# Attention then a bilinear feed-forward on one core: the first batch's softmax is normalised after the value product instead of before it

## The chip, the core and the metric

The kernel runs on one core of a Trainium2 chip. The core has a matrix engine (PE, with its weight loads shown as PEld), a vector engine (DVE), a scalar engine (ACT), a general engine (POOL) and a queue engine (SP) that issues most transfers. The metric is the device time of one execution in microseconds (us). PE reads the on-chip memory and writes only PSUM; DVE and ACT bring results from PSUM back.

## The reference

```python
scores = q @ k.T / sqrt(64); decay = cum[:, None] - cum[None, :]      # cum = cumsum(log(f))
attn = exp(scores + decay - max), with the causal mask
attn = attn / (attn.sum(-1) + 1e-9)
x = attn @ v                          # 8 batches, 8 heads, 576 rows, 64 per head
out = ((x @ w_a) * (x @ w_b)) @ w_out # 4608 tokens, 512 -> 1536 -> 512
```

Inputs and outputs are float32, and the kernel computes in float16 with float32 sums.

## The kernel before

The work is cut into head pairs: `t` counts them from 0 to 31, four to a batch, so `t = 0` to `3` is batch 0 and `4` to `7` batch 1. Rows of a head are in five blocks `i` (four of 128 and one of 64). For each `t` and `i` the steps are:

- PE makes scores (`qk_group`), DVE takes their row maximum (`do_max`, L488; from batch 3 on `do_decay`), ACT the exponential with its row sum (`do_exp`, L550 and L544 for `i = 4`) into the tiles PA and PB (P), some of which lie in tiles of other names (`spread`, `S`);
- DVE makes the reciprocal of the sum (`do_recip`, L559 and L557, kept in `st`), and POOL multiplies P by it, one instruction for each head and block (`do_norm`, L567);
- P is transposed: in batch 0 by PE (`pe_tr`, L591, with an eviction by DVE or ACT), in the others by a DMA from SP's queue (`do_tr`, L583). PE multiplies by V (`do_pv`, L623; `do_pv4`, L636, for block 4), and DVE or ACT evicts the result into `xT` (`do_ev`, `do_ev4`).

The transposed tile has the keys on the partitions and the rows of the softmax along its free axis. Beside this stands the feed-forward, by runs of tokens: `psa` and `psb` (the gate products, L874), a copy of one (ACT or DVE), their product `ht` on DVE (L890), and the output `pso` (L899). The weights come in pieces by DMAs that POOL issues (L365): first 512 columns of `w_a` and of `w_b`, then 1024 of each (the large pieces), then `w_out`. The fifth gate product, `psa` of block 4 of the first run, is the first that needs the large piece of `w_a`.

Nothing is scheduled while it runs: every step is one `op` with its dependencies, `ORDER` lists all of them in a hand-over order, and `CHOICE` gives the engine of those that may go to several. Each engine executes its instructions in that order; so an instruction that waits holds up all behind it on its engine, loads and weight DMAs among them. Rings of tiles bound how far ahead a step may go: 4 PSUM tiles `ff` for all products but the scores, 3 tiles `n32` for loaded inputs, 2 tiles `osb` for outputs. Forty `fill` steps put matmuls without use on PE.

## Time and profile before

| what | before |
|---|---|
| time of the runs | 402.16 us median of 3 (401.61 to 402.33) |
| profiled execution: span from first to last instruction | 400.7 us |
| instructions | 11076 |
| PE, DVE busy in the span | 383.2 us (96%), 315.3 us (79%) |
| POOL, ACT busy | 253.6 us (63%), 250.0 us (62%) |
| mean granted PE clock | 0.986 |

The profile is of one execution, whose span is the only time known of it. It has several views: busy time of each engine in a stretch, with granted clock (1.00 is full) and the mean busy share of the 16 DMA engines (above 1 where transfers overlap); who waited for whom, with total, count and longest wait; groups of instructions by line and shape with busy total and mean duration in ns; the instructions in order of time (start, duration); and the chain of work that ended last. Matmul ends are modelled, so spacing says more of them than duration.

### The profile page before, as it was taken

The numbers are of one execution on the slowest core, as the hardware profiler recorded it, in microseconds if no ns is written. First come the engines' busy times: TensorE is split into PE (matmuls) and PEld (weight loads), VectorE is DVE, ScalarE is ACT, GpSimd is POOL, SyncE is SP. The second block draws the span as 40 slices with busy tenths as digits, with TensorE's granted clock in tenths as the row PEclk, the third lists the DMA queues.
The fourth block names the chain that finished last, engine by engine and source line by source line (L and its number), as shares of the span: only waits on it lengthen the run. The fifth ranks groups of instructions, "written<-read, shape, count | busy, mean of one in ns | idle before, by whom it ended". The sixth has DMA issues, their size and how long they took to land.

```text
span 400.7 us, 11076 instructions
## 1 busy us (share of the span) xinstructions
PE 383.2 (96%) x4040; PEld 212.0 (53%) x4040; DVE 315.3 (79%) x907; ACT 250.0 (62%) x757; POOL 253.6 (63%) x424
## 2 busy tenths in 40 slices
PE   8598799998999999999999999999999999999996
PEld 7466576765855544454445454544444444444553
DVE  8989798976778988997988889898969892373560
ACT  5798766666667778758785777577868673300011
POOL 3889876887397876897896849787968553000000
PEclk9889999998999999999999999999999999999999
DMA  7999989989999999999999999999997729000102
GB/s 282 240 186 289 204 177 224 213 150 215 208 301 208 227 171 330 201 277 212 295 187 286 211 255 273 233 241 190 276 187 218 157 66 202 28 2 36 71 0 79
DMA packets 148311, 78.22 MB, mean 195 GB/s; under 512 B 130592, under 2 KB 133408, under 8 KB 148256
## 3 DMA queue, kind: packets, MB, share of 16 engines
q1 hardware_dynamic: 144272, 72.53, 77.4%
q0 software_dynamic: 3696, 4.72, 7.0%
q8 instruction: 31, 0.51, 0.5%
q10 hardware_dynamic: 288, 0.26, 0.2%
q14 instruction: 24, 0.20, 0.1%
HBM read 49.69 MB, written 9.58 MB: 148 GB/s over the span
## 4 chain that ended last, share of the span: by engine, by line
PE 79%; DMA 9%; DVE 4%; POOL 2%; ACT 2%; issue 2%; SPq 0%; POOLq 0%; DVEq 0%; ACTq 0%
PE pso L899 22%; PE psa L874 22%; PE psb L874 21%; PE sc L401 8%; DMA wa<-in_moe_w_a_dram 5%; PE pv L611 2%; DVE st L488 2%; DMA k<-in_k_dram 1%; PE pv L613 1%; PE sc L636 1%; DMA PTB<-spread 1%; DMA PTB<-PB 1%; DVE qT L302 1%; PE pv L623 1%; ACT PB L550 1%
## 5 line engine op out<-in xcount | busy, mean ns | idle before, releaser
L874 PE MATMUL psa<-xT,wa 128*128 128x512 f16 (+2 forms) x528 | 116.2, 343 | 2.3 <-DMA wa<-in_moe_w_a_dram 1.7
L874 PE MATMUL psb<-xT,wb 128*128 128x512 f16 (+2 forms) x528 | 116.2, 343 | 0.1
L899 PE MATMUL pso<-wout,ht 128*128 128x512 f16 (+1 forms) x444 | 98.4, 374 | 0.0
L567 POOL TENSOR_SCALAR PA<-PA,st 128x128 f16<-128x128 f16 (+2 forms) x162 | 76.0, 482 | 31.8 <-DVE st L559 20.4
L890 DVE TENSOR_TENSOR ht<-psb,a 128x512 f16<-128x512 f32 (+2 forms) x132 | 76.2, 589 | 22.0 <-PE psb L874 15.0
L512 DVE CUSTOM_DVE_ANT_0 S<-sc,spread 128x128 f32<-128x128 f32 (+3 forms) x160 | 86.7, 567 | 7.7 <-PE sc L401 5.4
L138 ACT CAST a<-psa 128x512 f16<-128x512 f32 (+2 forms) x85 | 43.5, 515 | 55.9 <-PE psa L874 53.8
L874 PEld LDWEIGHTS <-wa 128*128 128x128 f16 x528 | 50.1, 99 | 45.5 <-issue 3.7
L874 PEld LDWEIGHTS <-wb 128*128 128x128 f16 x528 | 50.4, 99 | 41.5 <-issue 1.7
L567 POOL TENSOR_SCALAR PB<-PB,st 128x512 f16<-128x512 f16 (+1 forms) x84 | 58.7, 712 | 15.7 <-DVE st L559 14.6
L550 ACT ACTIVATE PA<-S,st 128x256 f16<-128x256 f32 (+2 forms) x120 | 59.9, 502 | 12.5 <-DVE st L512 12.4
L899 PEld LDWEIGHTS <-ht 128*128 128x128 f16 x444 | 41.7, 98 | 46.8 <-issue 1.3
L488 DVE TENSOR_REDUCE st<-sc 128x2 f32<-128x512 f32 (+7 forms) x68 | 46.3, 723 | 6.0 <-PE sc L401 5.3
L401 PE MATMUL sc<-kT,qT 32*128 32x128 f16 (+5 forms) x960 | 41.7, 272 | 5.5 <-ACT PA L550 2.1
L550 ACT ACTIVATE PB<-S,st 128x512 f16<-128x512 f32 x40 | 28.5, 714 | 7.9 <-DVE st L512 7.9
L401 PEld LDWEIGHTS <-qT 32*128 32x128 f16 (+1 forms) x960 | 18.6, 96 | 26.7 <-issue 14.4
L142 DVE CAST a<-psa 128x512 f16<-128x512 f32 (+2 forms) x47 | 26.2, 560 | 7.2 <-PE psa L874 6.6
L559 DVE RECIPROCAL st<-st 128x2 f32<-128x2 f32 x128 | 18.5, 157 | 14.0 <-ACT PA L550 8.7
L142 POOL CAST k<-k 128x1152 f16<-128x1152 f32 (+1 forms) x15 | 20.5, 1367 | 8.9 <-DMA k<-in_k_dram 8.9
L138 ACT COPY osb<-pso 128x512 f32<-128x512 f32 (+1 forms) x22 | 12.4, 570 | 19.9 <-PE pso L899 15.1
L138 ACT CAST xT<-pv 128x512 f16<-128x512 f32 (+2 forms) x39 | 17.0, 446 | 11.8 <-PE pv L636 5.8
L140 POOL TENSOR_SCALAR q<-q 128x1152 f16<-128x1152 f32 (+1 forms) x15 | 20.6, 1372 | 5.0 <-DMA q<-in_q_dram 4.2
(98 smaller groups left out, 491.5 us busy)
## 6 DMA issues: line engine op xcount, KB each, us to landing
spread<-cum_d SPq DMA_DIRECT2D x20, 576.0 KB, 5.9
out_dram<-osb SPq DMA_DIRECT2D x35, 256.0 KB, 3.8
q<-in_q_dram SPq DMA_DIRECT2D x15, 576.0 KB, 7.3
k<-in_k_dram SPq DMA_DIRECT2D x15, 576.0 KB, 5.2
v<-in_v_dram SPq DMA_DIRECT2D x32, 256.0 KB, 6.1
wout<-in_moe_w_out_dram POOLq DMA_DIRECT2D x3, 512.0 KB, 8.7
v<-in_v_dram SPq DMA_DIRECT2D x8, 128.0 KB, 7.2
wb<-in_moe_w_b_dram POOLq DMA_DIRECT2D x1, 1024.0 KB, 13.5
```

What stands on the lines that cost most here:

```text
L138: nc.scalar.copy(out=out_, in_=in_)
L140: ENG[e].tensor_scalar(out=out_, in0=in_, scalar1=0.125, scalar2=1.0, op0=MUL, op1=MUL)
L142: ENG[e].tensor_copy(out=out_, in_=in_)
L401: nc.tensor.matmul(out=dst, lhsT=lhsT, rhs=rhs, start=start, stop=stop, skip_group_check=True)
L488: nc.vector.tensor_reduce(out=m if i == 4 else st[:, 2 * i:2 * i + 2][:, h:h + 1] if isinstance(x, list) else m, in_=y, axis=AXX, op=MAX, ...
L512: nc.vector.tensor_tensor_reduce(out=o, in0=x, in1=y, scale=-1.0, scalar=3e38, op0=ADD, op1=MIN, accum_out=m)
L550: nc.scalar.activation(out=p_blocks(t, i)[:, :, h, :], in_=x.rearrange("p (j k) -> p j k", k=128), func=EXP, scale=sign, bias=st[:, c:c + ...
L559: nc.vector.reciprocal(out=st[:, 20 + 2 * i:22 + 2 * i], in_=st[:, 10 + 2 * i:12 + 2 * i])
L567: ENG[e].tensor_scalar(out=p, in0=p, scalar1=st[:, c:c + 1], scalar2=1.0, op0=MUL, op1=MUL)
L874: nc.tensor.matmul(out=o, lhsT=w16[:, db, 128 * fb:128 * fb + 128], rhs=tokens(db, t0, n), start=(db == 0), stop=(db == 3))
L890: nc.vector.tensor_tensor(out=ht[:, 0:n], in0=T.pop(("psb", t0, fb))[:, 0:n], in1=T.pop(("a16", t0, fb))[:, 0:n], op=MUL)
L899: nc.tensor.matmul(out=o, lhsT=T[("ht", t0, fb)][:, 128 * tb:128 * tb + 128], rhs=wout16[:, fb, c], start=(fb == 0), stop=(fb == 11))
```

## The change

Only batch 0 (`RAW = 1`) changes in what it does. Its P is transposed and multiplied by V as the exponential left it. The 36 multiplications on POOL go. In their place, for each head pair and each of two groups of rows (blocks 0 and 1; blocks 2, 3 and 4):

- the reciprocals are split into a float16 high part and the rest (`rhi`, `rlo`, 4 or 5 columns; POOL, DVE or ACT);
- PE carries them across (`rmm`, 8 matmuls for the first group and 12 for the second): a column of reciprocals, repeated 64 times, times the unit matrix, so that every partition holds the reciprocals along the free axis; the two parts are added in PSUM, in a tile of the ring `ff`;
- ACT or DVE copies that to a tile `rb` of the ring `osb` (`rev`);
- the eviction of the value product becomes a multiplication by `rb`, on DVE alone (`ever`, `ev4r`).

The filler is one matmul over 512 columns in place of four over 128. `ORDER` and `CHOICE` are new for the first third: from the step after the third output run on (position 894 of 2311 before, 890 of 2307 now; on PE the last `psa` of the run of tokens from 768) all steps stand in the same order on the same engines. Ahead of it, loads, weights and steps of batches 0 to 2 have other places, and 36 steps another engine.

```diff
+    r16 = fixed("r16", [128, RAW * NP, 2, 10])
...
-        for n in range(4):
-            nc.tensor.matmul(out=p[:, 128 * n:128 * n + 128], lhsT=ident, rhs=ident, start=True, stop=True)
+        nc.tensor.matmul(out=p.rearrange("p (n k) -> p n k", n=4), lhsT=ident,
+                         rhs=ident.unsqueeze(1).to_broadcast([128, 4, 128]), start=True, stop=True)
...
+    def recip_high(e, t, lo, hi):
+        cast(e, r16[:, t, 0, lo:hi], T[("st", t)][:, 20 + lo:20 + hi])
+
+    def recip_low(e, t, lo, hi):
+        ENG[e].tensor_tensor(out=r16[:, t, 1, lo:hi], in0=T[("st", t)][:, 20 + lo:20 + hi], in1=r16[:, t, 0, lo:hi], op=SUB)
+
+    def across(t, rows):
+        o = T[("psr", t, rows[0])] = ps.tile([128, 512], FP32, tag="ff", bufs=RING["ff"], name="psr")
+        for i in rows:
+            c = slice(128 * (i - rows[0]), 128 * (i - rows[0]) + (64 if i == 4 else 128))
+            for e in range(2):
+                for h in range(2):
+                    r, x, n = (HP[h], 64 * h, 8) if i == 4 else (slice(0, 128), 0, 2 * i + h)
+                    nc.tensor.matmul(out=o[HP[h], c], lhsT=r16[r, t, e, n:n + 1].to_broadcast([r.stop - r.start, 64]),
+                                     rhs=ident[r, x:x + c.stop - c.start], start=i == rows[0] and e == 0, stop=e == 1,
+                                     skip_group_check=True)
+
+    def across_evict(e, t, rows):
+        n = 320 if 4 in rows else 256
+        x = T[("rb", t, rows[0])] = osb_pool.tile([128, 512], FP32, tag="osb", name="rb")
+        cast(e, x[:, 0:n], T.pop(("psr", t, rows[0]))[:, 0:n])
...
-        cast(e, xT[pr][:, b, c], T.pop(("pv", t, rows))[:, c])
+        o = T.pop(("pv", t, rows))
+        if b < RAW:
+            nc.vector.tensor_tensor(out=xT[pr][:, b, c], in0=o[:, c], in1=T[("rb", t, rows[0])][:, 0:256], op=MUL)
+        else:
+            cast(e, xT[pr][:, b, c], o[:, c])
...
+            if b < RAW:
+                norms.setdefault((t, part), []).extend((i, ex) for ex in es)
+                pair = (0, 1) if i < 2 else (2, 3, 4)
...
+                continue
             for h in range(1 if i == 4 else 2):
                 nm = op("P", f"norm{i}", lambda e, i=i, h=h: do_norm(e, t, i, h), [rc])
...
     ORDER = """
-        42-44 0 20 41 2 1 64 26 31 23 54 55 45 16 32 13 12 71 46 37 47 56 18 67 27 65 34 72 73 68 48 24 19
```

What stood in POOL's queue before around the large pieces (`wb16` and `wa16` with 1024 columns; PA and `spread2` are multiplications of P, `nv1` a cast of batch 1's V):

```order
L567 TENSOR_SCALAR PA_353<-PA_353,st_341 128x2x128 x2
L365 DMA wa16_70<-in_moe_w_a_dram 128x4x512
L567 TENSOR_SCALAR PA_374<-PA_374,st_370 128x2x128 x2
L365 DMA wb16_71<-in_moe_w_b_dram 128x4x512
L567 TENSOR_SCALAR PA_374<-PA_374,st_370 128x128
L142 CAST nv1_74<-v32_377 128x1024
L567 TENSOR_SCALAR spread2_80<-spread2_80,st_444 128x2x128
L365 DMA wb16_71<-in_moe_w_b_dram 128x4x1024
L365 DMA wa16_70<-in_moe_w_a_dram 128x4x1024
```

The same place now (`r16` holds the split reciprocals, `q16` and `k16` are batch 1's casts):

```order
L367 DMA wa16_70<-in_moe_w_a_dram 128x4x512
L144 CAST nv0_73<-v32_439 128x1024
L577 TENSOR_TENSOR r16_75<-st_364,r16_75 128x4
L144 CAST r16_75<-st_291 128x4
L577 TENSOR_TENSOR r16_75<-st_358,r16_75 128x4
L367 DMA wb16_71<-in_moe_w_b_dram 128x4x512
L144 CAST r16_75<-st_257 128x4
L577 TENSOR_TENSOR r16_75<-st_257,r16_75 128x4
L142 TENSOR_SCALAR q16_629<-q32_444 128x1152
L367 DMA wb16_71<-in_moe_w_b_dram 128x4x1024
L144 CAST k16_697<-k32_695 128x1152
L367 DMA wa16_70<-in_moe_w_a_dram 128x4x1024
```

The two large pieces now stand behind the split reciprocals of all four head pairs and behind a cast each.

SP's queue before, from the sixth transfer on (batch 0's V, then batch 1's and the first of batch 2):

```order
L288 DMA q_332<-in_q_dram 128x1152
L272 DMA v_355<-in_v_dram 128x8x64 x2
L272 DMA v_377<-in_v_dram 128x8x64 x2
L272 DMA v_380<-in_v_dram 128x8x64 x2
L288 DMA k_384<-in_k_dram 128x1152
L272 DMA v_690<-in_v_dram 64x8x64
L231 DMA cum_d<-cum_f 64x576
L288 DMA k_932<-in_k_dram 128x1152
L288 DMA q_1035<-in_q_dram 128x1152
L288 DMA q_1050<-in_q_dram 128x1152
```

And now (`k_414` is the second half of batch 1's k, `k_932` before; `q_1232` the first half of batch 2's q, `q_1035` before):

```order
L274 DMA v_278<-in_v_dram 128x8x64 x2
L290 DMA k_414<-in_k_dram 128x1152
L274 DMA v_439<-in_v_dram 128x8x64 x2
L290 DMA q_444<-in_q_dram 128x1152
L274 DMA v_564<-in_v_dram 64x8x64
L290 DMA k_695<-in_k_dram 128x1152
L274 DMA v_720<-in_v_dram 64x8x64
L233 DMA cum_d<-cum_f 64x576
L274 DMA v_1082<-in_v_dram 128x8x64 x2
L290 DMA q_1098<-in_q_dram 128x1152
L290 DMA q_1232<-in_q_dram 128x1152
```

The second half of batch 1's k moved ahead of three loads, the first half of its V behind four, and batch 2's q behind both.

DVE's queue before, where the first four value products are evicted (`psP` are transposes):

```order
L488 TENSOR_REDUCE st_370<-sc2_576 128x2
L559 RECIPROCAL st_444<-st_444 128x2
L142 COPY xT3_69<-psP_626 128x768
L142 COPY xT0_66<-psP_647 128x768
L142 COPY xT2_68<-psP_654 128x768
L559 RECIPROCAL st_341<-st_341 128x2
L559 RECIPROCAL st_437<-st_437 128x2
L559 RECIPROCAL st_341<-st_341 128x2
L142 CAST xT3_69<-pv_675 128x256
```

And now:

```order
L490 TENSOR_REDUCE st_291<-sc2_489 128x2
L577 TENSOR_TENSOR r16_75<-st_291,r16_75 128x4
L490 TENSOR_REDUCE st_257<-sc2_490 128x2
L144 COPY rb_544<-psr_535 128x256
L144 COPY xT2_68<-psP_547 128x768
L668 TENSOR_TENSOR xT1_67<-pv_570,rb_544 128x256
L668 TENSOR_TENSOR xT3_69<-pv_589,rb_566 128x256
L144 COPY xT0_66<-psP_598 128x768
```

A transpose's eviction went to ACT, a split and a copy of carried reciprocals came, and the evictions of values became products.

More of the change, by code (lines that the diff above doesn't have):

```diff
@@ L71 @@
     EARLY = 2
+    RAW = 1
     T = {}
@@ L641, in do_ev @@
         c = slice(128 * rows[0], 128 * rows[-1] + 128)
-        cast(e, xT[pr][:, b, c], T.pop(("pv", t, rows))[:, c])
+        o = T.pop(("pv", t, rows))
[3 more added lines that the diff above has]
+            cast(e, xT[pr][:, b, c], o[:, c])
     def do_ev4(e, t):
         b, pr = divmod(t, NP)
-        cast(e, xT[pr][:, b, SF:S], T.pop(("pv4", t)))
+        o = T.pop(("pv4", t))
+        if b < RAW:
+            nc.vector.tensor_tensor(out=xT[pr][:, b, SF:S], in0=o, in1=T[("rb", t, 2)][:, 256:320], op=MUL)
+        else:
+            cast(e, xT[pr][:, b, SF:S], o)
     last_row = [[] for _ in range(RING["bc"])]
+    raw = {}
     ev_ops, late, last_pb = {}, {}, [[] for _ in range(RING["PB"])]
@@ L721, in softmax @@
             st_users[t].extend(es + [rc])
+            if b < RAW:
+                norms.setdefault((t, part), []).extend((i, ex) for ex in es)
+                pair = (0, 1) if i < 2 else (2, 3, 4)
+                raw.setdefault((t, pair), []).append(rc)
+                if len(raw[(t, pair)]) < len(pair):
+                    continue
+                x = (2 * pair[0], 9 if 4 in pair else 4)
+                rh = op("PDA", "rhi", lambda e, x=x: recip_high(e, t, *x), raw[(t, pair)], x[1] - x[0])
+                rl = op("PD", "rlo", lambda e, x=x: recip_low(e, t, *x), [rh], x[1] - x[0])
+                st_users[t].extend([rh, rl])
+                rm = op("E", "rmm", lambda _, pair=pair: across(t, pair), [rh, rl, o_id], 320 if 4 in pair else 256)
+                ru = take(rm, "ff")
+                re_ = op("AD", "rev", lambda e, pair=pair: across_evict(e, t, pair), [rm], 320 if 4 in pair else 256)
+                ru.append(re_)
+                raw[(t, pair[0])] = re_, take(re_, "osb")
+                continue
             for h in range(1 if i == 4 else 2):
@@ L845, in values @@
             pvu = take(pv, "ff")
-            ev = op("DA", "eve", lambda e, rows=rows: do_ev(e, t, rows), [pv])
+            ev = op("D" if b < RAW else "DA", "ever" if b < RAW else "eve", lambda e, rows=rows: do_ev(e, t, rows), [pv])
+            if b < RAW:
+                ev.deps.append(raw[(t, rows[0])][0])
+                raw[(t, rows[0])][1].append(ev)
             pvu.append(ev)
@@ L853, in values @@
         us = take(pv4, "ff")
-        ev4 = op("DA", "ev4", lambda e: do_ev4(e, t), [pv4])
+        ev4 = op("D" if b < RAW else "DA", "ev4r" if b < RAW else "ev4", lambda e: do_ev4(e, t), [pv4])
+        if b < RAW:
+            ev4.deps.append(raw[(t, 2)][0])
+            raw[(t, 2)][1].append(ev4)
         us.append(ev4)
@@ new lines @@
+        234 235 132 133 262 263 167 212 213 107 108 4 52 220 272 273 53 248 249 221 92 182-184 150 190 191
+        1594-1596 268 269 1598 1600 185 216 217 168 91 87 270 88 186 187 1597 1599 1601 1602 1604 197-199
+        205 206 3 173 178 286 180 63 179 174-176 299 305 300 301 307 154 287 293 1603 207 1606 1605 1608
+        1607 1609 214 215 218 242 219 288 295 243 94 230 289 181 306 222 294 188 93 224 336 189 278 225 231
+        308 1610 302 1611 1612 337 1614 338 223 1613 1616 172 343 1615 339 1618 1620 1619 1622 1621 344 256
@@ new lines @@
+        458 1699 473 461 476-478 414 504 506 420 1651 421 505 360 1700 1701 479 1702 1703 335 455 495 411
+        355 434 415 451 329 433 412 462 482 483 418 1705 1706 510 511 1707 452 463 419 484 1708 507 323 424
+        436 437 512 354 486 427 401 428 405 386 435 440 441 438 439 488 514 1710 457 1711 1714 1715 1712
+        1713 487 489 1716 1718 1719 1722 1720 380 515-517 1721 1723 1724 524 1725 474 536 537 502 1717 1726
+        1728 381 426 431 425 429 430 459 468 564 570 432 481 480 469 1727 1730-1732 1729 1733-1737 503 538
```

81 lines of the change are left out of this document (43 added, 38 removed), and 119 rows, old and new, of the table ORDER.

## Prediction

> **What bounds the kernel now.** First the page and busy time by stretch: which engine is full, and where.
>
> ```profile
> span 400.7 us, 11076 instructions
> ```
> ```profile
> core 0: us, PE busy (x) PEld busy (x) DVE busy (x) ACT busy (x) POOL busy (x), PEclk, DMA share, GB/s
> 0.00:44.20 44.20, 33.20 (x563) 26.24 (x563) 39.72 (x101) 33.56 (x107) 33.85 (x61) 0.92 1.01 248
> 44.20:62.00 17.80, 17.76 (x288) 12.81 (x289) 15.52 (x29) 12.06 (x35) 12.58 (x19) 1.00 0.96 188
> 62.00:92.00 30.00, 29.16 (x480) 20.38 (x482) 25.95 (x67) 20.68 (x76) 24.59 (x42) 1.00 1.03 193
> 92.00:100.00 8.00, 6.22 (x88) 4.63 (x82) 4.13 (x9) 4.90 (x14) 5.10 (x10) 0.79 1.10 210
> 100.00:137.20 37.20, 36.75 (x501) 23.75 (x501) 29.96 (x83) 25.66 (x87) 26.90 (x43) 1.00 1.07 240
> 137.20:310.00 172.80, 172.75 (x1559) 80.69 (x1558) 151.61 (x506) 126.75 (x375) 134.84 (x225) 1.00 1.00 237
> 310.00:390.00 80.00, 80.00 (x528) 39.27 (x527) 47.78 (x115) 24.86 (x65) 15.71 (x28) 1.00 0.31 72
> ```
>
> At 137.2 stand the last feed-forward products of the part whose order changes; all behind it keeps its order. There PE is busy for 172.75 of 172.80 us and then 80.00 of 80.00, at full clock: the tail is matmul time alone, and it shifts as a block with PE's arrival at it. So the change is worth what it does to PE before 137.2. There PE idles 11.0 us up to 44.2 and 3.1 behind (0.04, 0.84, 1.78, 0.45), and from 92 to 100 its clock is 0.79, which costs 0.21 x 8 = 1.7 us more. Up to 44.2 no engine is full, but DVE is the nearest (39.72 of 44.20, and its first microsecond waits for the program's start); POOL with its 33.85 has room. Who ends PE's waits:
>
> ```profile
> PE sc L401 <- ACT PA L550: 2.1, 1, 2.1
> PE sc L401 <- DVE st L559: 2.1, 1, 2.1
> PE pv L636 <- DMA PTB<-spread: 1.8, 1, 1.8
> PE psa L874 <- DMA wa<-in_moe_w_a_dram: 1.7, 1, 1.7
> PE pv L636 <- DVE st L488: 0.8, 1, 0.8
> ```
>
> No wait ends at POOL's multiplication (L567), though POOL's work is what the change removes. The chain that ended last says the same: it runs through DVE's transposes and maxima, then through one weight transfer, and from there along PE.
>
> ```profile
> 22.51 21.65 DMA wa<-in_moe_w_a_dram
> 44.21 0.61 PE psa L874 x4
> ```
>
> **The change part by part.**
>
> *POOL's multiplications of the first batch go: 36.*
>
> ```profile
> L567 POOL TENSOR_SCALAR spread<-spread,st 128x128 f16<-128x128 f16 x4 | 1.5, 376 | 0.8 <-DVE st L559 0.8
> L567 POOL TENSOR_SCALAR spread<-spread,st 128x576 f16<-128x576 f16 x2 | 1.5, 744 | 0.9 <-DVE st L557 0.9
> ```
>
> The smallest took 0.376 and the largest 0.744; at their mean, 0.56, that is 20 us of POOL. All of it lay beside DVE and ACT, so by itself it is worth nothing on the end: DVE is late next.
>
> *Term A: the start of the fifth gate product (44.21).* POOL also issues the weights, and their place in its queue moves.
>
> ```profile
> 21.95 0.16 DVE L559 RECIPROCAL st<-st 128x2 f32<-128x2 f32 x1
> ```
> ```profile
> 21.71 0.81 POOL L365 DMA_DIRECT2D wb<-in_moe_w_b_dram  x1
> 22.51 0.75 POOL L365 DMA_DIRECT2D wa<-in_moe_w_a_dram  x1
> ```
> ```profile
> L142 POOL CAST k<-k 128x1152 f16<-128x1152 f32 x2 | 2.8, 1395 | 0.0
> ```
>
> Before, the two large pieces go out at 21.71 and 22.51. Now POOL first waits for the last reciprocal of rows 0 and 1 (ends at 22.1 by the row above), does some four tiny operations on it (taken at 0.15 each, like the reciprocal; POOL's smallest row, 0.376, would add 0.9), the small wb piece (0.8), and a q cast (1.4): wb's large piece at 22.1 + 0.6 + 0.8 + 1.4 = 24.9, 3.2 later. Behind it a k cast of 1.4 and the issue of 0.8: wa's large piece at 27.1, 4.6 later. Against that stand the loads in its way.
>
> ```profile
> q1 hardware_dynamic: 5108, 3.63, 39.4%
> ```
> ```profile
> 28.25 0.35 SPq L288 DMA_DIRECT2D k<-in_k_dram  x1
> 31.86 3.51 SPq L288 DMA_DIRECT2D q<-in_q_dram  x2
> ```
>
> From 14 to 46 us the loads' queue takes 39.4% of 32 us for 3.63 MB, 3.5 us a MB, so 2.0 us for a load of 0.59 MB. Three such loads start during wa's 21.65 us. SP's new order has one of them (batch 1's second k) ahead of all weights, and one (batch 2's q) behind batch 1's v and q: two leave, 4.1 us. Landing: 44.16 + 3.2 - 4.1 = 43.3, if the weights' queue works in order; ends: 40.1 (the loads leave and the later issue costs nothing) and 27.1 + 21.65 = 48.8 (the transfer keeps its length). I take 43.3, since queue and loads together fill the DMA engines (share 1.01 in the first row of the stretches).
>
> Does PE arrive by then? Its last row before the wait, and two groups from the chain behind it:
>
> ```profile
> 42.12 0.44 PE L591 MATMUL psP<-ident,PB 128*128 128x128 f16 x5
> ```
> ```profile
> 45.26 0.69 PE sc L401 x28
> 46.49 0.28 PE pv L636 x10
> ```
>
> PE is done at 42.56. The new order puts a score group (0.69) and a value group (0.28) ahead of the fifth gate product, and moves one transposition group (about 0.44) behind it: 0.53 more done. DVE up to there loses a subtraction and a q cast, two evictions of transposes and three casts of values, and gains a transpose and the products:
>
> ```profile
> L302 DVE STREAM_TRANSPOSE kT<-k 128x576 f32<-128x576 f32 x8 | 9.7, 1214 | 0.0
> L220 DVE TENSOR_TENSOR wout<-cum_f,wout 32x320 f16<-32x320 f32 x1 | 1.0, 1035 | 0.0
> L140 DVE TENSOR_SCALAR q<-wout 128x512 f16<-128x512 f32 x1 | 1.2, 1158 | 0.0
> L142 DVE COPY xT<-psP 128x768 f16<-128x768 f16 x7 | 3.7, 546 | 0.0
> L142 DVE CAST xT<-pv 128x256 f16<-128x256 f32 x6 | 2.4, 408 | 0.0
> L890 DVE TENSOR_TENSOR ht<-psb,a 128x256 f16<-128x256 f32 x36 | 14.7, 418 | 6.5 <-ACT a L138 2.6 <-PE psb L874 2.5 <-PE pv L623 0.6
> ```
>
> Gone: 1.04 + 1.16 + 3 x 0.41 and about 1.2 for two evictions (0.55 and a larger one), 4.6. Come: 1.21, five products of PSUM and SBUF, priced by the feed-forward's product of the same size (0.42; the last is shorter), one copy of 0.4, three tiny ones of 0.15 and one eviction of 0.5: 4.6. No gain and no loss; a product with a float32 second operand stands in no row, and lies between the cast (0.41) and double that. The first four products also wait for copies of the carried reciprocals, three of them queued on ACT between exponentials; behind them on DVE stand the maxima of row 4, and for those PE's first feed-forward products leave time. PE then arrives at 42.56 + 0.53 = 43.1 and starts at 43.3: 0.9 earlier with 0.53 more behind it, **A = -1.4** (ends -1.6 with no wait, +4.1 with 48.8).
>
> *Term B: the matmuls that carry the reciprocals across.* For each head pair 8 and 12; 44 stand ahead of the fifth gate product, in the stretch where PE idles 11 us, and cost nothing while it does (36 ns each, 1.6 us, if that cover goes). 36 stand behind it, on the full PE.
>
> ```profile
> 65.37 0.51 PE pv L623 x14
> 108.25 0.43 PE sc L636 x20
> 80.34 0.22 PE idle L178 x4
> ```
>
> Values products of the same shape (64 output rows, 128 columns) take 0.51 / 14 = 36 ns each; with 64 columns 22 ns; a full 128 x 128 one in the filler 55 ns. **B = 36 x 36 ns = +1.3** (0.8 to 2.0).
>
> The Trainium skill (TensorE: Matmul & The Clock Gate, "Back-to-back issue gap") gives about 81 ns a matmul for a stream of weight loads and matmuls at 128 columns; as an estimate, B by it would be 2.9 us and the forecast 1.6 later. The trace does not agree: 36 ns in the row above.
>
> *Term C: PE's waits and slow clock from 44.2 to 137.2*, 3.1 and 1.7. The wait of 1.8 is for the transpose of the last head pair's rows 3 and 4, issued behind two others of pair 6; now it is issued ahead of one of these, and the matmuls that use pair 6's come two gate products later. The wait of 0.8 stands between two small value groups; one of them now comes four products later. Behind the long wait PE ran slow:
>
> ```profile
> 67.21 0.60 PE L874 MATMUL psb<-xT,wb 128*128 128x256 f16 x4
> 96.30 1.06 PE L874 MATMUL psb<-xT,wb 128*128 128x256 f16 x4
> ```
>
> If that wait goes the clock loss should go too. But PE comes earlier, and a new wait of one transfer may open elsewhere. I take half of 4.8: **C = -2.4**; ends -4.8, and +2.1 for one more wait like the two longest in the waits above.
>
> The Trainium skill (same page, "The HAM clock gate") lets the clock fall after an idle window of about 3.4 us; by it a wait of 1.8 would cost no clock, and C as an estimate -1.5. The trace shows the granted 0.79 right around a wait of 1.8.
>
> *The rest.* 40 fillers stay, of the same columns; 7 of them stand behind the fifth gate product before, and 7 now: 0. The evictions of products that move from ACT to DVE and back are priced in the second rival. The tail: 0.
>
> **Sum**: -1.4 + 1.3 - 2.4 = -2.5. The profiled span of 400.7 becomes 398.2; the median of the runs, 402.16, lies 1.5 above that span, and I keep the distance: **399.7 us**.
>
> **The rivals.**
> 1. *Slower: the weights come late.* wa's large piece is issued 4.6 us later and still needs its 21.65. PE waits at the fifth gate product until 48.8: A = +4.1, and with B and C +3.0, 405.2. It decides from a landing at 45.8 on, where A is +1.1 and the sum nought. For it: the transfer is the longest link of the chain. Against it: two of three loads leave its way. 14%.
> 2. *DVE becomes the bound.* All twelve products of values now run on DVE, where before eight of these evictions were ACT's. Their 8 x 0.42 = 3.4 fall mostly between 44 and 92, where DVE is busy 41.47 of 47.8 us; if a third of its 6.3 idle can be used, 1.3 shows on PE, and C's gain is lost: 402.16 - 1.4 + 1.3 + 1.3 = 403.4. Against it: the moved evictions of transposes go to ACT. 12%.
> 3. *A wash.* A and C only change their place, B eats what is left: 401.5 to 402.9. For it: nothing on PE's chain is removed as such. 18%.
> 4. *More is gained.* All of C goes and A reaches its end: -1.6 + 0.8 - 4.8 = -5.6, 396.6. 12%.
> 5. The change does what it says: no multiplication of the first batch is left on POOL. No chance is kept for the opposite.
>
> **How the numbers follow.** The forecast (397.5 to 401.3) has 44%. Faster by over 0.2% (0.8 us, about what a measurement of this kernel can tell from no change) are the forecast and rival 4: 56%. Within it rival 3 and a little of rival 2: 20%. Slower the rest: 24%. The range of 8 in 10 reaches below rival 4's 396.6 (A, B and C at their best ends) and up to just short of rival 1's 405.2, so that some half of that one and the outermost ends are left out: 395.8 to 404.6.
>
> **What would show it.** A: the fifth gate product (psa's first wait on wa) starts at 43 to 44, and wa's large transfer is issued near 27 and takes about 16 us; 48 is rival 1. B: the new line's matmuls near 36 ns apart. C: the waits of PE on PTB transposes between 44 and 137 total under 2 us, and the clock stays at 1.00 from 92 to 100. The tail: PE busy throughout, and the psa that began at 119.95 begins some 2.5 us sooner. Wrong would be the whole if the tail showed waits of PE: then another engine carries it once PE is early.

## The result and the profile after

| | kernel before | changed kernel |
|---|---|---|
| median of 4 executions | 402.25 us | 406.18 us (404.74 to 410.57) |
| ratio to the kernel before, 95% interval | 1 | 1.0107 (1.0066 to 1.0148) |
| again (e14) | 402.71 us (35 executions) | 405.93 us (399.92 to 410.94; 12 executions) |
| profiled execution, span | 400.7 us | 405.21 us, span 403.4 us |

A ratio leaves out executions over 1.5% above the fastest of their kernel; the changed kernel scatters by more than that, so that e14's ratio, 1.0027 (0.9987 to 1.0068), leaves out half of its twelve, and the medians of all stand beside ratios below. The changed kernel is slower by 3 to 4 us in the median, while its best execution is as fast as one of the kernel before. The kernel before ran again beside every set of experiments, at medians from 401.64 to 402.71 us, and each ratio is to the kernel before of its own set.

Busy time by stretch of the changed kernel (columns as in the prediction):

```profile
0.00:44.20 44.20, 37.40 (x526) 22.02 (x530) 38.50 (x96) 34.36 (x110) 20.75 (x40) 0.85 1.02 232
92.00:100.00 8.00, 7.62 (x170) 5.76 (x168) 6.11 (x17) 5.03 (x14) 6.88 (x13) 1.00 1.12 180
118.00:128.00 10.00, 10.00 (x84) 5.91 (x82) 9.32 (x31) 7.83 (x27) 8.81 (x12) 1.00 1.22 225
128.00:132.00 4.00, 0.94 (x24) 0.65 (x24) 1.81 (x5) 0.38 (x2) 1.48 (x4) 0.90 1.35 183
132.00:136.00 4.00, 4.00 (x48) 2.38 (x44) 2.34 (x12) 2.51 (x8) 2.45 (x6) 0.67 1.19 273
140.00:310.00 170.00, 169.60 (x1545) 79.19 (x1542) 148.40 (x494) 124.16 (x369) 131.85 (x221) 1.00 1.03 238
```

POOL is relieved (33.85 to 20.75 us up to 44.2), and from 92 to 100 the clock is back at 1.00. New is the stretch from 128 to 136: PE works 0.94 of 4 us, and then at a clock of 0.67. PE in order of time there, and the chain of waits that leads to it:

```profile
130.35 0.35 PE L660 MATMUL sc<-PTB,nv 128*64 128x64 f16 x10 [2.07 <-DMA PTB<-PB]
131.69 0.48 PE L660 MATMUL sc<-PTB,nv 128*64 128x64 f16 x10 [0.99 <-DMA PTB<-PB]
```
```profile
121.09 1.36 POOL PB L569 x2
122.45 0.53 issue
...
125.35 6.29 DMA PTB<-PB
131.64 0.04 issue
131.69 0.48 PE sc L660 x10
```

These are the P-times-values matmuls of head pairs 10 and 11; they wait 3.06 us for the transposes of PB. SP's queue, first of the changed kernel, then of the kernel before (start, time on the queue):

```profile
116.46 0.84 SPq L458 DMA_DIRECT2D spread<-cum_d  x1
117.40 0.41 SPq L290 DMA_DIRECT2D k<-in_k_dram  x1
119.12 2.28 SPq L607 DMA_TRANSPOSE PTA<-PA  x1
121.50 7.21 SPq L607 DMA_TRANSPOSE PTB<-PB  x2
```
```profile
116.56 3.73 SPq L583 DMA_TRANSPOSE PTA<-PA  x2
120.35 1.01 SPq L288 DMA_DIRECT2D k<-in_k_dram  x1
122.65 5.05 SPq L583 DMA_TRANSPOSE PTB<-PB  x2
```

The first transpose of PB of these pairs went out 1.15 us earlier than before, but the two held the queue for 7.21 instead of 5.05 us; in the trace they landed at 130.31 and 131.64 (before: 127.68 and 130.43).

How far PE stood from the kernel before is read off DVE's 132 feed-forward products, whose number is the same in every kernel: start of the n-th (from 0) less its start in the kernel before, in us, minus is ahead. (Up to product 36 the two orders differ in what PE has done by the n-th product: at 9 the changed kernel is 12 transposes and 4 gate-product matmuls short of the kernel before, at 12 it has 28 score and 20 value matmuls more. At 39 all kernels of the table have done the same, but for the 80 matmuls that carry reciprocals.) The columns e3 to e16 are kernels of the experiments.

```
  n   before   changed    e3     e5     e9    e13    e14    e16
  3    42.95    -1.24  -3.90  -3.77  -1.21  -3.72  -2.21  +0.69
  9    55.03    -1.72  -4.38  -4.09  -1.64  -3.61  -2.68  -0.90
 12    68.69    +1.95  -0.60  +0.43  +2.04  +0.06  +4.08  -0.91
 27   103.03    -3.14  -1.97  -3.89  -3.29  -2.79  +1.08  -4.88
 39   126.18    -1.57  -1.97  -2.53  -1.66  -1.47  +2.64  -3.95
 42   129.96    -1.97  -1.84  -2.92  -2.05  -1.88  +2.25  -3.27
 45   136.85    +2.50  -0.37  +0.63  -0.01  +0.18  +3.38  -2.28
 78   244.14    +2.74  +3.03  +0.54  -0.17  +0.19  +6.22  -2.88
end   400.69    +2.76  +3.06  +0.58  -0.12  +0.24  +6.28  -2.96
```

The changed kernel is 2.0 us ahead at 130 us and loses 4.5 in the next 7.

### The profile page after: what moved, and what is told of

It reads as the page before. It is cut to its first block, busy times and chain, and to the rows that moved or that the text cites. A ratio compares the mean times of both kernels' runs of the same rounds, so it can differ in the third digit from the quotient of the medians.

```text
span 403.4 us, 10967 instructions
## 1 busy us (share of the span) xinstructions
PE 388.1 (96%) x4000; PEld 207.8 (51%) x4000; DVE 317.4 (79%) x927; ACT 250.4 (62%) x749; POOL 237.6 (59%) x400
## 4 chain that ended last, share of the span: by engine, by line
PE 76%; DMA 7%; DVE 5%; POOL 4%; ACT 3%; issue 3%; SPq 1%; POOLq 0%; ACTq 0%; DVEq 0%
PE pso L954 22%; PE psb L929 19%; PE psa L929 19%; PE sc L403 8%; DMA PTB<-PB 4%; DVE st L490 3%; PE pv L635 2%; DMA v<-in_v_dram 2%; PE psP L615 2%; POOL PB L569 1%; PE pv L637 1%; PE sc L660 1%; DMA PTB<-spread 1%; PE psr L586 1%; ACT spread L552 1%
## 5 line engine op out<-in xcount | busy, mean ns | idle before, releaser
L929 PE MATMUL psb<-xT,wb 128*128 128x512 f16 (+2 forms) x528 | 115.5, 341 | 1.0 <-ACT a L140 0.6
L929 PE MATMUL psa<-xT,wa 128*128 128x512 f16 (+2 forms) x528 | 115.2, 341 | 0.1
L569 POOL TENSOR_SCALAR PA<-PA,st 128x128 f16<-128x128 f16 (+2 forms) x150 | 69.8, 478 | 40.9 <-DVE st L561 28.0
L929 PEld LDWEIGHTS <-wb 128*128 128x128 f16 x528 | 50.2, 98 | 43.1 <-issue 3.5
L929 PEld LDWEIGHTS <-wa 128*128 128x128 f16 x528 | 50.0, 98 | 43.0 <-issue 3.0
L140 ACT CAST a<-psa 128x512 f16<-128x512 f32 (+2 forms) x77 | 40.3, 528 | 50.9 <-PE psa L929 48.8
L569 POOL TENSOR_SCALAR PB<-PB,st 128x512 f16<-128x512 f16 (+1 forms) x78 | 54.2, 708 | 10.7 <-DVE st L561 7.5
L490 DVE TENSOR_REDUCE st<-sc 128x2 f32<-128x512 f32 (+8 forms) x68 | 46.7, 725 | 9.9 <-PE sc L403 9.2
L144 DVE CAST a<-psa 128x256 f16<-128x256 f32 (+2 forms) x55 | 29.5, 539 | 6.8 <-PE psa L929 6.0
L144 POOL CAST nv<-v 128x1024 f16<-128x1024 f32 (+1 forms) x24 | 21.4, 894 | 12.8 <-DMA v<-in_v_dram 12.5
L142 POOL TENSOR_SCALAR q<-q 128x1152 f16<-128x1152 f32 (+2 forms) x16 | 21.9, 1369 | 8.8 <-DMA q<-in_q_dram 8.2
L140 ACT COPY osb<-pso 128x512 f32<-128x512 f32 (+1 forms) x24 | 13.5, 572 | 19.3 <-PE pso L954 15.8
L552 ACT ACTIVATE PA<-sc,st 128x256 f16<-128x256 f32 (+2 forms) x42 | 19.6, 492 | 9.4 <-DVE st L490 6.8
```

What stands on the lines that cost most here:

```text
L140: nc.scalar.copy(out=out_, in_=in_)
L142: ENG[e].tensor_scalar(out=out_, in0=in_, scalar1=0.125, scalar2=1.0, op0=MUL, op1=MUL)
L144: ENG[e].tensor_copy(out=out_, in_=in_)
L490: nc.vector.tensor_reduce(out=m if i == 4 else st[:, 2 * i:2 * i + 2][:, h:h + 1] if isinstance(x, list) else m, in_=y, axis=AXX, op=MAX, ...
L552: nc.scalar.activation(out=p_blocks(t, i)[:, :, h, :], in_=x.rearrange("p (j k) -> p j k", k=128), func=EXP, scale=sign, bias=st[:, c:c + ...
L569: ENG[e].tensor_scalar(out=p, in0=p, scalar1=st[:, c:c + 1], scalar2=1.0, op0=MUL, op1=MUL)
```

## The experiments

**e1: the two loads ahead of the transposes go elsewhere.**

```diff
 SP's order
   spread, pair 12
+  spread, pair 15
...
-  spread, pair 15
-  k, batch 3, heads 4 to 7
   PTA, pair 11
   PTB, pair 10
   PTB, pair 11
+  k, batch 3, heads 4 to 7
```

> The changed kernel with two loads of 576 KB moved in SP's order: the spread rows of pair 15 go out right behind those of pair 12 (as before the change), and the second k load of batch 3 behind the last PTB transpose of pair 11. Theory 1 (the two loads, issued at 116.46 and 117.40, take the DMA engines from the transposes of pairs 10 and 11, which then take 3.75 and 3.36 us on SP's queue and land at 130.3 and 131.7): the transposes take about 2.5 us each again, land near 127.7 and 129.8, the wait of the P-times-values matmuls of pairs 10 and 11 falls from 3.1 to at most 1.3 us, the clock stays above 0.9 behind it, and the time falls from 406.2 (405.2 in the profiled run) by 2 to 4.5 us, to 401 to 403. Theory 2 (the chain DVE, POOL, SP, transposes of these pairs runs at its own pace and PE only came 2 us earlier to it): the transposes land at 130 to 131.7 as now, wait and time stay: 404.5 to 406. Theory 3 (the k load is then late for POOL's cast and the next pairs): the wait goes, but POOL waits for k and the loss comes back behind 132: 404 to 407.

Measured: 410.0 us (407.96 to 411.34). PE's longest wait of e1, and its busy time behind 128:

```profile
PE sc L660 <- DVE st L514: 4.8, 1, 4.8
```
```profile
128.00:132.00 4.00, 2.34 (x23) 1.37 (x22) 0.06 (x1) 0.98 (x3) 0.00 (x0) 1.00 0.96 271
```

The time lies above the ranges of all three theories. Theories 1 and 3 were both right in part: the transposes held the queue for 1.8 and 2.1 us, but left only at 122.7 and 124.5 and landed at 129.0 and 130.4; and behind them the k load left at 126.7 and landed at 132.2. POOL, held up by the cast of k, did nothing for 4 us (0.00), DVE waited for POOL, and PE for DVE, 4.8 us. The loads stand where they stand because the next pairs need them.

**e2: PE has other work in that place.**

```diff
 PE's order
   psa fb 7
+  psb fb 7, psa fb 8, psb fb 8
   pv4 pair 10; pv4 pair 11; pv pair 11
   next score group
-  psb fb 7, psa fb 8, psb fb 8
```

> The changed kernel with PE's order altered in one place: one psa and two psb products of the run from token 768 (the psb of fb 7, psa and psb of fb 8: 12 matmuls, about 2.0 us) go ahead of the P-times-values matmuls of pairs 10 and 11 instead of behind them; loads and transposes stay. Theories 1 and 2 alike (PE's wait for these transposes, and the clock behind it, are the loss): the wait falls from 3.1 to about 1.1 us, the clock stays above 0.9 from 128 to 136, and the time falls by 2 to 3.7 us, to 401.5 to 404 against 406.2 (405.2 in the profiled run). Theory 4 (the wait is only where a loss shows that is set by something else, such as the decay rows and exponentials of pairs 12 and 13, which wait for the same score tiles): what is taken off here comes back as a wait at the next score group within 10 us, and the time stays at 405 to 406.5.

404.36 us (403.64 to 408.55), ratio 1.0087 (1.0042 to 1.0133). The profiled execution was late before it came there (a wait of 2.47 us for an earlier transpose, at 109.81); from product 42 to 45 it then lost 1.4 us instead of 4.5, with a wait of 1.04 at the next score group. Part of the wait moves on, as theory 4 had it.

**e3 and e4: which part of the order carries the loss.** Both kernels are put together from the two orders; the new work of the change ends within the first 450 operations.

```diff
 e3:  changed kernel, operations 0 to 449
-     changed kernel, the rest
+     the same operations as the kernel before has them
 e4:  kernel before, operations 0 to 449
-     kernel before, the rest
+     the same operations as the changed kernel has them
```

> The changed kernel as far as the last operation that the change adds (450 operations), and behind it all remaining operations in the order, and on the engines, of the kernel before. Theory 1 (the order around 110 to 130 put the loads in front of the transposes): the transposes take 2.3 to 2.7 us on SP's queue again and land by 129 or so, PE waits under 1 us for them, and the gain of 2.0 us that the changed kernel has at 118 us lasts to the end: 399.5 to 401.0 against 402.2 of the kernel before. Theory 2 (the chain of pairs 10 and 11 has its own pace): transposes land at 130 as in the kernel before, PE waits up to 2 us there, and the time is the kernel before's: 401.7 to 403.5. Theory 5 (the gain at 118 us is due to the moved order behind the first batch, not to what the change does in the first batch): no lead at 118 us, 402 to 404.

> The kernel before as far as 450 operations, and behind it all remaining operations in the order, and on the engines, of the changed kernel: P is normalised on POOL as before the change, only the later order is new. Theory 1 (the loads ahead of the transposes make them late): the transposes of pairs 10 and 11 take over 3 us on SP's queue and land at 131 to 132, PE waits 1 to 3 us there and its clock falls below 0.9 behind it: 403 to 406 against 402.2 of the kernel before. Theory 2 (only PE's earlier arrival made the wait): PE arrives at about 130 and waits under 0.5 us: 401.5 to 402.7.

e3: 405.82 us, 1.0101 (1.0054 to 1.0148). e4: 400.70 us, 0.9982 (0.9952 to 1.0013). **The loss is in the first part, the gain in the second** (e4's interval still holds no change; that of e16 below, the same kernel, does not). Theory 1, which put the loss on the later order, falls; e3's time lies above every range given for it. e3 lost 1.5 us at 128 (waits of 0.41 and 1.07, clock 1.00) and 3 more at 212 to 220, to the same kind of wait and the clock behind it:

```profile
212.83 0.35 PE L660 MATMUL sc<-PTB,nv 128*64 128x64 f16 x10 [0.77 <-DMA PTB<-PB]
...
214.82 0.35 PE L660 MATMUL sc<-PTB,nv 128*64 128x64 f16 x10 [1.09 <-DMA PTB<-PB]
```
```profile
212.00:216.00 4.00, 2.14 (x53) 1.75 (x56) 1.83 (x5) 0.79 (x4) 1.73 (x4) 0.91 1.02 213
216.00:220.00 4.00, 4.00 (x27) 1.59 (x28) 2.63 (x10) 3.18 (x11) 2.12 (x3) 0.66 1.11 385
```

**e5 and e6: where the tiles lie.** r16 takes 160 bytes of each partition, and the program's addresses show every tile behind it (PB from 100992 to 101152, PTB from 192640 to 192800) 32 bytes off a multiple of 64.

```diff
 e5 (of the changed kernel)
-    r16 = fixed("r16", [128, RAW * NP, 2, 10])
+    r16 = fixed("r16", [128, RAW * NP, 2, 12])
 e6 (of the kernel before)
+    gap = fixed("gap", [128, 80])
...
         make_identity(nc, ident)
+        nc.gpsimd.memset(gap, 0.0)
```

> The changed kernel with 32 more unused bytes per partition in the tile of the reciprocals: r16 is 192 bytes long instead of 160, so that the 50 or so tiles that are placed behind it (PB, spread, the loads' targets, PA, PTA, PTB) begin at a multiple of 64 bytes again, as in the kernel before; with 160 bytes they all begin 32 bytes off one. Not an instruction is altered. Theory 6 (the tile's length moved the others off their alignment, and the DMA transposes became slower: of their 256-byte packets between 60 and 330 us, 81 and 80 in 100 take 18 ns in the two kernels without r16, but 76 to 78 in 100 in the four with it): this share is 80 or more again, the transposes of pairs 10 and 11 land before 130, the wait there is under 1.5 us, and the time is 400 to 402.5 against 406.2 (405.2 in the profiled run). Theory 2 (PE's lead of 2 us runs into a stretch in which the DMA engines set the pace, and the wait costs clock on top): nothing changes, 405 to 407.

> The kernel before with an unused tile of 160 bytes per partition at the place where the changed kernel has r16 (POOL sets it to zero once, behind the identity at the start), so that all tiles behind it begin 32 bytes off a multiple of 64. Order and work are those of the kernel before. Theory 6 (alignment): 76 to 78 in 100 of the transposes' packets take 18 ns instead of 81, waits for transposes of PB appear on PE, and the time is 403.5 to 406.5 against 401.6 to 402.2. Theory 2 (PE's lead meets the DMA's pace): nothing changes, 401 to 402.7.

e5: 403.77 us, 1.0035 (1.0005 to 1.0065), against 1.0107 without the 32 bytes. e6: 403.36 us, 1.0032 (1.0004 to 1.0059). Both move as theory 6 said, by less: some 1.2 us in the kernel before, at the edge of what can be told. That the transposes are the way is not shown. e6's trace is 1.4 us behind already at product 3, where no DMA transpose has gone out yet, 0.6 at product 12 and 1.5 at the end; and the share of the transposes' packets at 18 ns, 78.9 and 78.6 in 100, lies between the two groups (e16 below, without r16, has 78.9). And e5 does not end the story: its trace loses the same way at 128 us, waits of 0.80 and 1.07 and then

```profile
130.00:132.00 2.00, 2.00 (x32) 1.22 (x29) 0.49 (x3) 1.49 (x5) 0.73 (x3) 0.50 1.34 213
132.00:134.00 2.00, 2.00 (x10) 1.02 (x9) 2.00 (x9) 0.82 (x3) 2.00 (x4) 0.71 0.93 321
```

a clock of 0.50 and 0.71, 1.6 us.

**e7: the new work alone, in the old order.**

```diff
 operations of the kernel before, with
-  norm0 to norm4 of batch 0, eve, ev4
+  rhi, rlo at the last norm of a group; rmm, rev ahead of pve; ever, ev4r for eve, ev4
```

> The order and the engines of the kernel before, with the change's other work alone: the first batch's normalisations on POOL go, the reciprocals' high and low parts stand where the last of them stood, the carry matmuls stand just ahead of the P-times-values matmuls, their evictions on ACT, and the products' evictions multiply on DVE; r16 has 192 bytes. Theory 7 (the gain at 118 us comes with the moved order, not with the work that is saved on POOL): PE's starts stay where the old order puts them, the carry matmuls come on top, and no lead arises: 402 to 405. Theory 8 (POOL's normalisations were what the first batch waited for): a lead of 1 to 2 us at 118 us without any move, and 399.5 to 401.5.

e7, in which part of the tiles `rb` also lie in `spread` instead of the ring `osb`, computes a wrong result, for a reason that was not found. Its 411.5 us say nothing, and whether the work pays without any move stays open.

**e8 to e11: holding the clock, and PE's order once more**, all on e5.

```diff
 PE's order
 e8, e11
+  5 idle matmuls of 512 columns
   first rows product
 e10
+  4 idle matmuls of 512 columns
   pv4 pair 10
+  4 idle matmuls of 512 columns
   pv4 pair 11
 e9, e11: as e2
```

> The changed kernel with r16 of 192 bytes (e5) and 5 more idle matmuls of 512 columns (0.22 us each at full clock) ahead of the first rows product, where PE waits 1.9 us till 8.40 in the changed kernel and 0.96 us in e5. Theory 9 (that wait is what lets the clock fall: 0.57 from 8 to 12 us and 0.50 from 20 to 28 in the changed kernel, but 1.00 in both stretches in e5, and the first products come 2.5 us later for it): the clock is 0.85 or more from 20 to 28 in this run, and the fourth gate product is evicted 3.5 to 4 us ahead of the kernel before. What is left of that at the end: theory 2 (PE meets the transposes of pairs 10 and 11 at 128 whatever its lead) says 402.5 to 404.5 against 403.8 of e5; the rival (an earlier start pays through to the end) says 400.5 to 402.

> e5 (r16 of 192 bytes) with PE's order of e2: psb of fb 7, psa and psb of fb 8 of the run from token 768 (2.0 us) ahead of the P-times-values matmuls of pairs 10 and 11, where e5's profile shows waits of 0.80 and 1.07 us and behind them a clock of 0.50 to 0.71 from 130 to 134 (1.6 us lost). Theory 2 (PE's lead of 2.9 us at 130 is lost to this wait and the clock behind it): waits there under 0.5 us, clock 0.95 or more from 128 to 136, and 400 to 401.5 against 403.8. Theory 4 (something else paces this stretch): the lead at 137 us is still within 0.7 us of the kernel before, and the time 403 to 405.

> e5 (r16 of 192 bytes) with 4 idle matmuls of 512 columns ahead of the P-times-values matmuls of pair 10 and 4 ahead of those of pair 11 (8 times 0.22 us = 1.7 us, about the 1.9 us that PE waits there in e5's profile). They do no work: what they can give is the clock alone. Theory 10 (the wait makes the clock fall, and the fall costs as much as the wait): clock 0.95 or more from 128 to 136, the wait's 1.9 us stay as fillers, and the time falls by 1 to 1.7 us, to 402 to 403 against 403.8. Rival (the clock falls there for another reason, or the fillers make PE late where it would not have waited): 403.5 to 405.5.

> e8 and e9 together: r16 of 192 bytes, 5 more idle matmuls early, and 2.0 us of PE's work ahead of the P-times-values matmuls of pairs 10 and 11. If theories 2 and 9 hold: a lead of 2.5 to 3.5 us at 128 us of which at least 2 us last to the end, 399 to 401 against 402.2 of the kernel before. If theory 4 holds: 402.5 to 405.

| | median of 12 | ratio, 95% interval |
|---|---|---|
| e8 | 406.40 us (401.80 to 410.38) | 1.0059 (1.0018 to 1.0100) |
| e9 | 402.63 us (400.81 to 406.58) | 1.0032 (0.9999 to 1.0066) |
| e10 | 406.12 us (402.18 to 412.16) | 1.0057 (1.0020 to 1.0095) |
| e11 | 405.55 us (400.97 to 410.02) | 1.0042 (1.0004 to 1.0080) |

None of the four times lies in a range that was given for it. In place the edits show more. Early clock of the changed kernel and of e8:

```profile
8.00:12.00 4.00, 3.60 (x47) 1.49 (x46) 3.23 (x3) 3.02 (x6) 3.15 (x10) 0.57 1.13 287
20.00:24.00 4.00, 3.68 (x58) 2.02 (x58) 2.68 (x13) 4.00 (x17) 3.17 (x8) 0.50 1.03 230
```
```profile
8.00:12.00 4.00, 2.70 (x49) 1.31 (x48) 2.87 (x3) 2.96 (x5) 2.17 (x4) 1.00 1.11 311
20.00:24.00 4.00, 2.84 (x70) 1.76 (x67) 3.21 (x14) 4.00 (x17) 3.15 (x8) 1.00 1.12 262
```

and e10 at pairs 10 and 11, with PE filled and the clock at 1.00:

```profile
128.00:132.00 4.00, 4.00 (x25) 2.17 (x23) 3.58 (x9) 2.57 (x11) 3.24 (x5) 1.00 1.18 170
132.00:136.00 4.00, 4.00 (x64) 2.26 (x63) 2.59 (x10) 1.91 (x6) 1.57 (x5) 1.00 1.28 231
```

From product 42 to 45, e5 lost 3.6 us, e8 3.8, e10 1.9 (the 1.7 of its fillers), e9 2.0, e11 1.4. In e5 the wait (1.87) and the clock behind it (1.6) are two losses of about the same size. That fillers hold the clock is not shown by e10: it came there 4 us later than e5, and by the landings (131.45 and 132.85) PE would have waited some 1.2 us without them, while waits of 1.06 (e14), 1.48 (e3) and 1.95 us (e16) cost no clock. Nor does it take a lead over the kernel before: e8 came there 3.0 us behind it, its transposes landed at 134.35 and 135.67, PE waited 2.17 us, and the clock fell:

```profile
136.00:138.00 2.00, 2.00 (x37) 1.10 (x31) 0.85 (x4) 1.46 (x5) 0.55 (x2) 0.58 1.44 227
138.00:140.00 2.00, 2.00 (x8) 0.96 (x7) 2.00 (x9) 0.71 (x2) 2.00 (x5) 0.57 0.88 293
```

But e8, e10 and e11 had lost more already, between 55 and 69 us. POOL in order of time, the cast of batch 1's v, in the changed kernel and in e8:

```profile
46.14 1.04 POOL L144 CAST nv<-v 128x1024 f16<-128x1024 f32 x1 [7.69 <-DMA v<-in_v_dram]
```
```profile
52.48 1.04 POOL L144 CAST nv<-v 128x1024 f16<-128x1024 f32 x1 [12.89 <-DMA v<-in_v_dram]
```

In the eleven traces that have the change's first batch and its order behind, v landed either at 41 to 49 us, and then 3.7 to 4.5 us of lead went from product 9 to 12 (3.7 in five of them, which is what the order puts there), or at 51.1 to 52.4 (e8, e10, e11, e14), and then 6.8 to 8.1 went: POOL casts q only behind v, DVE turns q only then, and PE waits for DVE (`PE psb L929 <- DVE xT L668`, 1.9 to 3.0 us in these four). That is 3 us and more between one trace and another.

**e12 to e15: the loads of w_out.** Without the normalisations POOL reaches its three loads of w_out (512 KB each in the tile by the profile, not 0.8 MB as the expectations have it) at once:

```diff
 POOL's order, e12 and e13 (e13 with e9's order of PE)
-  three loads of w_out
...
   cast of v, batch 1
+  two loads of w_out
...
   cast of q, batch 1
+  third load of w_out
 e14: the changed kernel
 e15 (of the kernel before)
   norm2 of pair 3
+  three loads of w_out
```

> e5 (r16 of 192 bytes) with the three loads of wout moved in POOL's order: two stand behind the cast of the second batch's first v piece, the third behind the cast of its second q piece, instead of ahead of both. Theory 11 (POOL, free of the normalisations, issues the three loads, 0.8 MB each, in a burst at 34.6 to 37 us, and the v and q loads of the second batch, issued at 30.0 and 34.3, share the DMA engines with them and land 16 and 14 us later): v lands at 38 to 42 and q at 40 to 45 us, DVE and PE have no wait for q between 54 and 60 us, and the time is 400.5 to 402.7 against 403.8 of e5, with less scatter. Theory 2 alone (whatever is gained ahead of 118 us is lost at pairs 10 and 11): 403 to 405. Risk of the move: wout lands later than the first pso products want it at 57 us, then PE waits there for DMA wout.

> e9 (r16 of 192 bytes, 2.0 us of PE's work ahead of pairs 10 and 11) with e12's place of the wout loads. If theories 2 and 11 both hold: no waits over 0.7 us at 54 to 60 and at 128 to 132 us, and 399.5 to 401.7, faster than the kernel before. If the DMA engines' pace behind 60 us sets the time whatever comes before: 402 to 404, like e9.

> The changed kernel itself once more, as it is, beside e12, e13 and e15 on one chip. Theories 2, 6 and 11 alike: 404 to 407 and a scatter of 4 us or more; its profile shows the v load of the second batch landing at 45 to 53 us, and waits for the PTB transposes.

> The kernel before with its three loads of wout moved ahead in POOL's order, in one burst behind the first normalisation of rows 2 of pair 3 (about 34 us), where the changed kernel issues them, instead of at 38.1, 44.3 and 46.5 us. Theory 11 (the burst makes the second batch's loads late): q and v of the second batch land 3 us or more later than 39.1, 43.1 and 47.0, and the time is 403 to 406 against 402.2. Rival (the loads have slack there, and the changed kernel's loss comes from elsewhere): 401.5 to 402.7.

| | median of 12 | ratio, 95% interval | first piece of batch 1's v lands |
|---|---|---|---|
| e12 | 404.03 us (400.83 to 406.88) | 1.0025 (0.9988 to 1.0062) | 43.7 us |
| e13 | 402.81 us (399.71 to 408.00) | 1.0005 (0.9973 to 1.0036) | 41.3 us |
| e14 | 405.93 us (399.92 to 410.94) | 1.0027 (0.9987 to 1.0068) | 51.8 us |
| e15 | 401.52 us (400.19 to 406.97) | 0.9980 (0.9951 to 1.0008) | 17.2 us, second piece 54.2 |

From 30 to 46 us, the DMA queues of e14 and of e13 (packets, MB, share of 16 engines; software is POOL's weights, hardware SP's loads):

```profile
q0 software_dynamic: 1639, 2.53, 86.3%
q1 hardware_dynamic: 2471, 0.94, 28.4%
```
```profile
q0 software_dynamic: 781, 1.49, 51.3%
q1 hardware_dynamic: 2707, 1.91, 43.1%
```

With the burst the weights hold 86% of the engines and SP's loads move half as much. The Trainium skill (DMA: Bandwidth & Descriptors, "Queues, rings and completion order") says that an engine turns between its queue rows packet by packet; the trace agrees in that neither queue waits for the other to end, and it shows who loses. Moved, the loads let v land 8 to 10.5 us earlier than in e14, and no wait over 0.3 us is left from 54 to 60. In the kernel before the same burst costs nothing (e15). There the first piece of batch 1's v, the one that the changed order waits for, went out ahead of all weights and had landed at 17.2; the halves of k and q that batches 1 and 2 need next land at 35.7 to 42.0; and only the second piece of v, wanted later, lands at 53.3 and 54.2 (48.9 and 55.5 without the burst). For the landings, theory 11 holds in the changed order alone, where v stands ahead of q on POOL. For the time it is not shown: e12 (404.03) and e13 (402.81) lie in the ranges of its rivals, no lower than e5 and e9 with the burst (403.77 and 402.63), and their executions spread over 6.1 and 8.3 us, those of e5 and e9 over 5.7 and 5.8. With alignment, burst and PE's order mended (e13), the median of all executions is level with the kernel before, as e9's is with alignment and PE's order alone. What e13's profiled execution still waits for behind 62 us:

```profile
PE pv L660 <- DMA PTB<-PB: 1.4, 1, 1.4
...
PE sc L660 <- DMA PTB<-PB: 1.3, 3, 0.6
...
PE pv L660 <- DMA PTB<-spread: 1.2, 1, 1.2
```

transposes, at 78, 94, 106 and 131 us, 3.5 us in sum up to there; 0.9 for DVE comes behind them.

**e16 to e18: the order without the change.**

```diff
 e16: e4 once more
 e17: e4 with e2's order of PE
 e18: e17 with e15's place of the w_out loads
```

> e4 once more, with more executions: the kernel before as far as 450 operations (P normalised on POOL, no r16), and the changed kernel's order behind. If the moved order behind the first batch is worth something by itself: 0.994 to 0.998 of the kernel before. If it is not: 0.999 to 1.003.

> e16 with PE's order of e2 and e9: 2.0 us of products ahead of the P-times-values matmuls of pairs 10 and 11, for which e4's profile shows waits of 0.60 and 1.10 us. Theory 2 (those waits are on PE's path): they go, and the time is 1.0 to 1.7 us under e16's. Theory 4 (what is gained there is lost at the next score group, as 0.86 us in e9 and 1.04 us in e2): within 0.7 us of e16.

> e17 with the three wout loads issued in one burst near 33 us, as in e15 (401.5 against 402.7 of the kernel before on its chip, 0.998 with an interval to 1.001). If e15's difference is real, 0.5 to 1 us under e17; if the burst makes the second batch's v loads late here, 1 to 3 us above it.

e16: 399.67 us, 0.9954 (0.9928 to 0.9981). e17: 400.33, 0.9962 (0.9934 to 0.9990). e18: 400.31, 0.9959 (0.9928 to 0.9991). **The moved order of batches 1 and 2, with P normalised on POOL as before, is faster than the kernel before, by 0.2 to 0.7%**, and so than the changed one; the two additions give nothing more. e16 has no wait over 0.3 us on PE between 42 and 126 us, arrives 3.3 us ahead at pairs 10 and 11 and waits there too,

```profile
PE sc L636 <- DMA PTB<-PB: 1.9, 2, 1.1
```

but its clock stays at 1.00 behind it and 2.3 us of the lead last:

```profile
128.00:132.00 4.00, 3.81 (x56) 2.41 (x56) 2.96 (x12) 3.13 (x11) 2.34 (x7) 1.00 1.12 227
140.00:310.00 170.00, 170.00 (x1553) 79.11 (x1552) 149.31 (x503) 125.88 (x374) 133.37 (x221) 1.00 1.00 239
```

From 62 to 118 us, e16 and e13 differ on PE (columns as in the prediction):

```profile
62.00:118.00 56.00, 55.41 (x890) 38.99 (x889) 46.83 (x113) 36.25 (x125) 43.18 (x72) 1.00 1.02 220
62.00:118.00 56.00, 52.47 (x843) 36.08 (x836) 43.53 (x108) 32.41 (x107) 38.57 (x64) 1.00 1.09 222
```

PE idles 0.6 us there in e16, and 0.5 in e4, e17 and e18. In the eleven traces with the changed first part and the same order behind it idles 1.4 (e9) to 5.2 us (e2), of which 0.6 to 4.5 are waits for transposes; in the kernel before, 3.1.

## Why the prediction was wrong

- **The tail** was forecast to shift as a block. In the profiled execution it did: the first output product behind it began at 141.00 instead of 138.50, and the end is 2.7 later. e3 and e14 show that this is not safe: e3 lost 3.4 us and e14 2.8 behind 205, with waits for transposes and, in e3, the clock behind them.
- **Term A** (-1.4) was mis-sized: the fifth gate product began at 44.61 with the 0.53 us more done, so A was -0.1.

```profile
30.66 1.39 POOL L144 CAST k<-k 128x1152 f16<-128x1152 f32 x1 [6.08 <-DVE qT L304]
32.00 0.75 POOL L367 DMA_DIRECT2D wa<-in_moe_w_a_dram  x1
```
```profile
44.61 0.61 PE L929 MATMUL psa<-xT,wa 128*128 128x256 f16 x4
```

The cause named was also wrong. wa's large piece was issued at 32.0, not 27, because the cast ahead of it waited 6.08 us for DVE's transpose of q, which the sum had left out. It still landed at 42.0, so PE did not wait for it, and rival 1 had no part. PE's half clock from 20 to 28 and DVE's maxima behind it (31 to 41 in the chain) set the start. That clock differs from one execution to the next: with 0.91 to 1.00 (e3, e5, e13) product 3 came 3.7 to 3.9 us early, not 1.2. e5 and e9 have the same instructions up to there; e9 came 1.2 early, at 0.50.
- **Term B** (+1.3) was right: behind the fifth gate product the groups of 12 carry matmuls took 0.40 to 0.52 us, 33 to 43 ns each, 1.4 in all.

```profile
49.98 0.40 PE psr L586 x12
...
60.55 0.52 PE psr L586 x12
...
62.94 0.52 PE psr L586 x12
```

The 81 ns that the Trainium skill gives (TensorE: Matmul & The Clock Gate, "Back-to-back issue gap") did not show.
- **Term C** (-2.4) is the step that failed. Its first half was more than right: the wait at 94 us fell from 1.77 to 0.38, the clock behind it went from 0.79 to 1.00, and up to 118 us C was -3.3 (waits and clock of 4.8 us before, waits of 1.5 now). The sentence "a new wait of one transfer may open elsewhere" was priced by the two longest waits of the kernel before. In fact PE met the transposes of pairs 10 and 11, 2 us early, while these landed 2.6 and 1.2 us late; the wait was 3.06, and the clock took 1.4 more: +4.5. So C was +1.2 in place of -2.4, and A + B + C = -0.1 + 1.4 + 1.2 = 2.5, the 2.5 us measured at 141.
- **The rivals.** None had this mechanism: PE, rid of its earlier waits, runs up to transfers that land no sooner, and the wait with the clock behind it takes more than was gained. How far PE is ahead of the kernel before does not decide it (e8 waited there though it was 3.0 us late); how far its own transposes are behind does. Rival 2 (DVE as the bound) was closest in sign, yet the waits are for transfers; DVE appears as a link behind q's cast. The remark that an earlier POOL changes where loads and weights stand was made for wa's large piece only; w_out's three were left out.
- **Fillers at 0** was too simple: the rows product's wait of 1.9 us, where fillers ended too soon, was followed by the 0.57 from 8 to 12 us. With five more fillers (e8, e11) the clock stayed at 1.00 up to 28 us; but so it did without them in e13, behind a wait of 1.25.

What is shown: the loss belongs to the first 450 operations of the changed kernel, its new work and their order together (e3 against e4 and e16). The lead at 118 us comes from the order of batches 1 and 2: e4, e16, e17 and e18 gain 3.0 to 3.1 us from product 12 to 39 with the first part of the kernel before, and lose their waits between 62 and 118. With the changed first part some of these waits come back, as waits for transposes (e13's 2.9 us). In the changed kernel's profiled execution few came back (PE idles 1.6 us there), and the loss is the 4.5 us at pairs 10 and 11.

What stays open: why PE has to wait for transposes between 62 and 118 behind the changed first part; what its moved loads have to do with it was not tried by itself. Whether the first part by itself brings PE a lead is not settled either: at product 12 the traces with it stand from 0.6 us ahead to 4.9 behind, those with the first part of the kernel before from 0.9 ahead to 2.3 behind, and the work done by then is not the same. Open too is how much of the loss is the 32 bytes: e8, e10 and e11 had them mended and medians of 405.6 to 406.4.
